# Two first-product blocks between the halves of G in the first batch, the gate's weights behind v, and a left-over pass whose strips hold column quarters

## The chip, the cores and the metric

The kernel runs on one core of one Trainium2 chip. The metric is the device time of one execution in microseconds. The core has a matrix engine (TensorE; PE for its matmuls and PEld for its weight loads in the profile), VectorE (DVE), ScalarE (ACT), GpSimd (POOL) and SyncE (SP), which issues nearly all of the transfers here.

## The reference

An attention with packed queries is followed by a mixture of experts with one expert per row.

```
p_packed = sm_attn(p, k, v)            # q, k, v: 8 batches x 8 heads x 576 x 64; p: 32 packed queries a head
x = sm_attn(q, p_packed, p_packed)     # each of the 576 rows attends to the 32 packed rows
x = x as 4608 rows x 512
e = argmax(x @ w_gate)                 # one of 8 experts a row
out[row] = gate_w[row] * sigmoid(x @ w_output_gate)[row, e] * (relu(x @ w1[e]) @ w2[e])
                                       # w1: 8 x 512 x 1024, w2: 8 x 1024 x 512
```

## The kernel before

Eight batches are worked through one after the other. For each of them `encode` computes the packed attention (scores `ps_s`, exponentials, their transposes `ps_a1T`, the product with v `ps_pp`), guesses one expert for the whole batch and loads its weights (`weights`); `route` computes the second attention up to its transposed weights, split into a high and a low part (`ah`, `al`), and the gate. `values_up` multiplies the packed values by the first weights of the guessed expert: G has two halves of 512 columns (`up(0)` and `up(1)`, 16 matmuls each), each lying in two PSUM banks (one for each group of heads), and `take_in` splits a bank into a high part on ScalarE (`Gh`, L76) and a low part on VectorE (`Gl`, L77). `ffn` then makes eight first-product blocks (`ps_h`, fc 0 to 7) of 128 rows of the hidden layer for each of two halves of the batch's rows. Blocks 0 to 3 read the first half of G, blocks 4 to 7 the second. Each is evicted as a rectified high part by ScalarE (L514) and a low part by VectorE (L517), and `product_out` multiplies by the second weights (`ps_o`, L556 and L571), which ScalarE and VectorE have split as well (L461, L463).

The order on every engine is written out by hand. `START` is a string of pieces done ahead of the first batch's `ffn`: `Y` and `y` step `encode`, `t` steps `route`, `W` steps `weights`, `G` steps `values_up`, digits are matmuls on zeros that keep TensorE busy, and `k`, `v`, `q` issue loads on SP's queue. `PLANS` has one string per batch; `8:WW` places two steps after the eighth step of that batch's `ffn`. In the first batch `values_up` gives way four times: after `up(0)`, after `up(1)`, and after either take-in. `START` has three of these steps (both products and the first take-in), and the plan's `1:G` does the second take-in behind block 0. PSUM has eight banks, four of which (tag "f") serve the warming matmuls, G of the first batch, the blocks `ps_h`, the outputs `ps_o` and the left-over pass. Before the second-layer weights are issued, GpSimd waits for the second chunk of the first ones (L172).

The loads are issued in the order of the string: k with the packed queries of the batch, then v, then q. Behind the second half of the first batch's k the gate's weights `wgo` (32 KB) are issued (L197, L198). They are first used in `encode(0)` at L274.

Rows whose expert is not the guessed one are left over. `first_leftover` treats one (row tile, quarter, expert) with 32 rows (`m` is 32) beside the last batch's `ffn`, at the letters `l` of the last plan; further ones go through a loop at the end, which runs no times with these inputs. With `m` = 32, `product` puts the 32-row partial products into four strips of 32 PSUM partitions, each strip with 512 columns and a fourth of the sum. The strips are added later, by the matrix `stack4`: for the hidden layer with eight products against it, which transpose at the same time (L687), and for the output with one more product (L697). Between the two stands the second layer's `product`. The row numbers (`ridi`) and scales (`vals`) are brought to 32 partitions by a product with `pick` (L643), and `scatter` writes 32 rows of 512 columns by an indirect transfer.

Of the kernel before, what the change touches and what calls it, by code (L numbers as in the profile page):

```python
# [19 lines left out]
P = 128  # L20
# [11 lines left out]
PLANS = ["1:G 4:WW 6:W 8:WW 9:tt 10:tWW 11:yy 12:Wyy 13:tt 14:ttty 15:ty 16:tyy 17:ty 19:yt 20:y 21:ryyr 22:yr 23:y "  # L32
# [9 lines left out]
def tile_packed_attn_then_moe(ctx, tc, qT, kT, v, pT, w_go, w1, w2, out):  # L42
# [131 lines left out]
    def fetch(x):  # L174

        queue = queues["kvq".index(x)]
        if not queue:
            return
        x, b, g = key = queue.pop(0)
        tag = "rq" if x == "q" else "raw"  # L180
        bufs = CFG[tag]
        if x == "v":
            t = sb.tile([P, T, NPAIR * D], F32, tag=tag, name="vt", bufs=bufs, **EVEN)
            if b == g == 0:
                after(nc.vector, t[0:1, 0, 0:1], loaded["k", 0, 0][0:1, 0, 0:1])
            nc.sync.dma_start(t, v[b, g])
        else:
            t = sb.tile([P, NPAIR, HS], F32, tag=tag, name=x, bufs=bufs, **EVEN)
            src = (kT if x == "k" else qT)[b, g]
            step = NPAIR // 2 if b == 0 else NPAIR  # L190
            for c in range(0, NPAIR, step):
                nc.sync.dma_start(t[:, c:c + step], src[:, c:c + step])
                if x == "k" and g == c == 0:
                    pt = sb.tile([P, NPAIR, NP], F32, tag="pt", name="pt", bufs=2)
                    nc.sync.dma_start(pt, pT[b])
                    loaded["p", b, g] = pt
        if key == ("k", 0, 1):  # L197
            nc.sync.dma_start(wgo, w_go)  # L198
        loaded[key] = t

# [268 lines left out]
    def values_up(b):  # L469

        w1s = W[b][0]
        ppT = packed[b]
        G[b] = []

        def up(n, tag):
            banks = [bank("ps_G", tag) for _ in range(NG)]
            by_head(banks, ppT, w1s[n * NPAIR:(n + 1) * NPAIR])
            return banks

        def take_in(banks):  # L480
# [6 lines left out]
        both = []  # L487
        for n in range(DF // BANK):
            both.append(up(n, "fa"[n] if b else "f"))
            if b == 0 or n:  # L490
                yield
        for banks in both:
            take_in(banks)
            yield

    def ffn(b):
        ah, al = A.pop(b)
# [83 lines left out]
    def leftover(nb=B, m=P):  # L581


        nq = P // m
        tags = dict(l_oh="raw", l_h="raw", l_some="row", l_a2="row", l_pp="row", l_o="ob", l_x="rq", l_hT="rq")

        def st(shape, nm, dt=F32, n=P):
            tag = tags.get(nm, nm)
# [44 lines left out]
        if m < P:  # L633
            here = st([Q], "l_q")
            nc.vector.tensor_reduce(here, oh.rearrange("p c q e -> p q c e"), axis=AX.XY, op=ALU.max)
            nc.vector.tensor_tensor(here, here, quarter[:, :, 0], ALU.mult)
            mine = st([1], "l_mine")
            nc.vector.tensor_reduce(mine, here, axis=AX.X, op=ALU.max)
            pick = st([m], "l_pick")
            nc.vector.tensor_scalar(pick, stack4, mine, None, ALU.mult)  # L640
            yield
            ps = bank("ps_lv", "f")[:m, :4]
            nc.tensor.matmul(ps, pick, vals, start=True, stop=True)  # L643
            vals = st([4], "l_valq", n=m)
            nc.vector.tensor_copy(vals, ps)
        ef = st([1], "l_ef", n=m)
        nc.vector.tensor_copy(ef, dec[:m, 0:1])
        nc.vector.tensor_tensor(ef, ef, vals[:, 0:1], ALU.not_equal)
        rid = st([1], "l_rid", n=m)
        nc.vector.scalar_tensor_tensor(rid, ef, no_row, vals[:, 2:3], op0=ALU.mult, op1=ALU.add)  # L650
        ridi = st([1], "l_ridi", I32, n=m)
        nc.vector.tensor_copy(ridi, rid)
        yield
        total = stack4 if m < P else ident
# [5 lines left out]
        for c in range(NPAIR):  # L660
            nc.scalar.copy(xT[:, c], pv[c])

        def product(ps, stat, wc):
# [10 lines left out]
        h = st([FC, P], "l_h")  # L674
        nf = BANK // P
        for n in range(DF // BANK):
            ps = bank("ps_lh", "f")
            yield from product(ps, xT, w1c[n * NG:(n + 1) * NG])
            nc.scalar.copy(h[:, n * nf:(n + 1) * nf], ps.rearrange("p (c n) -> p c n", n=P))
            yield  # L680
        hT = st([FC, m], "l_hT")
        for n in range(0, FC, BANK // m):
            fs = slice(n, min(FC, n + BANK // m))
            ps = bank("ps_lt", "f")
            pv = ps.rearrange("p (c n) -> p c n", n=m)[:, :fs.stop - fs.start]
            for c_ in range(fs.start, fs.stop):
                nc.tensor.matmul(pv[:, c_ - n], h[:, c_], total, start=True, stop=True)  # L687
            nc.scalar.activation(hT[:, fs], pv, AF.Relu)
        yield
        ps = bank("ps_lo", "f")  # L690
# [7 lines left out]
        ob = sb.tile([m, DM], F32, tag="ob", name="l_ob", bufs=CFG["ob"])  # L698
# [120 lines left out]
```

## Time and profile before

| | |
|---|---|
| median of 3 runs | 421.17 us (419.62 to 421.27) |
| profiled execution | 420.52 us |
| its span, first to last instruction | 418.8 us |
| mean granted TensorE clock | 0.993 of full speed |
| TensorE matmuls, busy | 404.1 us (96%) |
| VectorE, busy | 282.4 us (67%) |
| ScalarE, busy | 182.5 us (44%) |
| GpSimd, busy | 40.8 us (10%) |

The profiled execution is one of the kernel's executions, and its time is 1.7 us above its span. Sums over rows are made against 420.52. The times in all rows are microseconds from the start of the span.

### The profile page before, as it was taken

Reading aid. Unit: us, or ns where it says so; the run is one execution under the profiler, and the core shown is the slowest. Engines: PE = TensorE matmul, PEld = TensorE weight load, DVE = VectorE, ACT = ScalarE, POOL = GpSimd, SP = SyncE. Lnnn points to the kernel's source line nnn. Section 1 sums busy time; section 2 is a strip of 40 time slices with the busy share of each in tenths; the row PEclk is TensorE's granted clock in tenths of the full one; section 3 lists DMA queues with packets and bytes.
Section 4 is the critical chain, followed back from the end, with each engine's and each line's share of the span. In section 5 each row is a group of like instructions: output and inputs, shape, how many; then the busy total and the mean of one; then the engine's idle time right before and its main releaser. Section 6 shows DMA issues by size and latency. Waiting matters only on the chain.

```text
span 418.8 us, 9413 instructions
## 1 busy us (share of the span) xinstructions
PE 404.1 (96%) x3616; PEld 321.5 (77%) x3616; DVE 282.4 (67%) x810; ACT 182.5 (44%) x408; POOL 40.8 (10%) x36
## 2 busy tenths in 40 slices
PE   7979999899999999999999999999999999999994
PEld 4648877677868888788877888788977888798754
DVE  2659578585895776749774786749774786677610
ACT  2246425462467337342645337442645334533310
POOL 6000000260024200020002000020002000200010
PEclk9999999899999999999999999999999999999998
DMA  7999219920697079602992079602951077004801
GB/s 251 334 357 411 92 57 386 377 119 33 200 412 298 10 240 409 269 27 87 355 410 91 3 237 409 273 27 97 346 198 59 2 244 285 25 27 119 344 13 53
DMA packets 36686, 83.60 MB, mean 200 GB/s; under 512 B 3615, under 2 KB 16287, under 8 KB 36640
## 3 DMA queue, kind: packets, MB, share of 16 engines
q1 hardware_dynamic: 36608, 82.98, 54.2%
q8 instruction: 29, 0.48, 0.5%
q14 instruction: 17, 0.14, 0.1%
q0 software_dynamic: 32, 0.00, 0.0%
HBM read 67.76 MB, written 15.27 MB: 198 GB/s over the span
## 4 chain that ended last, share of the span: by engine, by line
PE 79%; DVE 1%; ACT 1%; issue 0%
PE ps_o L556 38%; PE ps_h L85 21%; PE ps_o L571 6%; PE ps_G L92 3%; PE ps_pp L92 2%; PE ps_s L92 2%; PE ps_s2T L92 2%; PE ps_a1T L240 1%; PE ps_lg L92 1%; ACT hT L514 1%; PE ps_lh L669 0%; PE ps_lo L669 0%; ACT a L231 0%; DVE Gl L77 0%; PE ps_lt L687 0%; PE ps_lg L85 0%
## 5 line engine op out<-in xcount | busy, mean ns | idle before, releaser
L556 PE MATMUL ps_o<-w2h,hT 128*128 128x512 f32 (+1 forms) x528 | 168.8, 391 | 0.1
L556 PEld LDWEIGHTS ps_o<-w2h,hT 128*128 128x128 f32 x528 | 98.2, 188 | 28.2 <-ACT Gh L76 5.0
L517 DVE SCALAR_TENSOR_TENSOR hT<-ps_h,hT 128x256 fp32r<-128x256 f32 x192 | 61.0, 352 | 65.4 <-ACT hT L514 65.0
L556 PE MATMUL ps_o<-w2l,hT 128*128 128x512 f32 (+1 forms) x264 | 101.4, 384 | 0.0
L85 PE MATMUL ps_h<-ah,Gh 128*128 128x256 f32 (+1 forms) x256 | 78.7, 308 | 1.2 <-DVE hT L517 0.7
L85 PE MATMUL ps_h<-al,Gh 128*128 128x256 f32 (+1 forms) x256 | 76.1, 297 | 0.0
L85 PE MATMUL ps_h<-ah,Gl 128*128 128x256 f32 (+1 forms) x256 | 76.0, 297 | 0.0
L514 ACT ACTIVATE hT<-ps_h 128x320 fp32r<-128x320 f32 (+1 forms) x128 | 51.4, 415 | 47.9 <-PE ps_h L85 47.2
L463 POOL TENSOR_TENSOR w2l<-wst,w2h 128x1024 fp32r<-128x1024 f32 x13 | 31.1, 2397 | 311.8 <-ACT w2h L461 281.7
L556 PEld LDWEIGHTS ps_o<-w2l,hT 128*128 128x128 f32 x264 | 49.7, 188 | 8.6
L85 PEld LDWEIGHTS ps_h<-ah,Gh 128*128 128x128 f32 x256 | 48.9, 191 | 6.2 <-DVE hT L517 1.8
L85 PEld LDWEIGHTS ps_h<-al,Gh 128*128 128x128 f32 x256 | 49.0, 191 | 0.2
L85 PEld LDWEIGHTS ps_h<-ah,Gl 128*128 128x128 f32 x256 | 49.0, 191 | 0.0
L538 ACT ACTIVATE ob<-ps_o,scm_all 128x512 f32<-128x512 f32 (+1 forms) x28 | 19.0, 680 | 37.2 <-PE ps_o L556 34.4
L461 ACT CAST w2h<-wst 128x1024 fp32r<-128x1024 f32 x32 | 33.4, 1069 | 3.2 <-PE ps_o L556 2.8
L463 DVE TENSOR_TENSOR w2l<-wst,w2h 128x1024 fp32r<-128x1024 f32 x19 | 23.2, 1220 | 6.3 <-ACT w2h L461 6.3
L77 DVE TENSOR_TENSOR Gl<-ps_G,Gh 128x512 fp32r<-128x512 f32 x32 | 20.1, 684 | 9.2 <-ACT Gh L76 9.1
L362 ACT CAST ah<-a2T 128x576 fp32r<-128x576 f32 (+1 forms) x18 | 11.2, 621 | 33.7 <-DVE a2T L356 33.7
L571 PE MATMUL ps_o<-w2h,hT 128*128 128x512 f32 x64 | 25.7, 401 | 0.1
L342 ACT ACTIVATE s<-s 128x576 f32<-128x576 f32 (+1 forms) x18 | 11.1, 629 | 29.9 <-DVE s L339 29.2
L571 PE MATMUL ps_o<-w2l,hT 128*64 128x512 f32 x64 | 23.9, 393 | 0.0
L231 ACT ACTIVATE a<-ps_s,nmx 128x288 f32<-128x288 f32 x32 | 15.8, 508 | 10.3 <-DVE nmx L226 9.5
(182 smaller groups left out, 446.0 us busy)
## 6 DMA issues: line engine op xcount, KB each, us to landing
w<-in_w_dram SPq DMA_DIRECT2D x36, 512.0 KB, 5.6
wst<-in_w_dram SPq DMA_DIRECT2D x36, 512.0 KB, 8.7
vt<-in_v_dram SPq DMA_DIRECT2D x16, 640.0 KB, 9.3
k<-in_kT_dram SPq DMA_DIRECT2D x14, 576.0 KB, 10.5
q<-in_qT_dram SPq DMA_DIRECT2D x14, 576.0 KB, 10.2
out_dram<-ob SPq DMA_DIRECT2D x31, 256.0 KB, 4.0
a_d<-a2T SPq DMA_DIRECT2D x16, 320.0 KB, 8.7
out_dram<-ob SPq DMA_DIRECT2D x10, 128.0 KB, 5.0
```

Of the source, the lines that this page charges most:

```text
L77: (lo_eng or nc.vector).tensor_tensor(lo, src, f(hi), ALU.subtract)
L85: res = nc.tensor.matmul(dst, a, m, start=j == 0, stop=j == len(seq) - 1)
L92: res = nc.tensor.matmul(dst, a, m, start=j == 0, stop=j == len(seqs[0]) - 1)
L231: nc.scalar.activation(a1[:, g, hf], s1[hf][g], AF.Exp, bias=nmx[g], scale=QK, accum_out=sm[:, g, hf:hf + 1])
L362: nc.scalar.copy(ah[:, g, ts], a2T[:, g, ts])
L461: nc.scalar.copy(hi, st)
L463: eng("w", b, j).tensor_tensor(lo, st, f(hi), ALU.subtract)
L514: nc.scalar.activation(hT[:, :n], ps, AF.Relu)
L517: nc.vector.scalar_tensor_tensor(hT[:, d0:d0 + s1 - s0], ps[:, s0:s1], 0.0, f(hT[:, s0:s1]), op0=ALU.max, op1=ALU.subtract)
L538: nc.scalar.activation(ob[:, cs], ps[:, cs], AF.Copy, scale=sc)
L556: nc.tensor.matmul(ps[:, cs], a, m[:, cs], start=fc == i == 0, stop=fc == FC - 1 and i == 2)
L571: nc.tensor.matmul(ps[:n], a, m, start=i == 0, stop=i == len(seq) - 1)
```

## The change

Three things are changed.

- In the first batch `values_up` now goes `up(0)`, take-in, `up(1)`, take-in, with a step after each. `START` has the first two, and the plan of the first batch has `2:GG` in place of `1:G`: the second product and its take-in stand behind blocks 0 and 1. The take-ins of this batch go by half banks: the first 256 columns of both banks, then the second 256. Other batches keep their order.
- The gate's weights are issued behind the second v load of the first batch instead of the second k load.
- In the left-over pass with 32 rows, `product` gives each strip of 32 partitions a quarter of the columns and the whole sum: four matmuls of 128 columns for each former one of 512. The hidden layer is rectified when it leaves PSUM, turned by two transposes of 128x128, and copied; the output needs no further product. `pick` now spreads row numbers and scales to all 128 partitions, each strip has its quarter's index added (`part`), and the scatter writes 128 pieces of 128 columns. The last step is one plan letter shorter.

```
-START = "kkvvqqkkYYYY1YY2YYY3YY4YYtYYWtttWYtttttttty6GGGvvqqkkvv"
+START = "kkvvqqkkYYYY1YY2YYY3YY4YYtYYWtttWYtttttttty6GGvvqqkkvv"
-PLANS = ["1:G 4:WW 6:W 8:WW 9:tt 10:tWW ...
+PLANS = ["2:GG 4:WW 6:W 8:WW 9:tt 10:tWW ...
...
-        if key == ("k", 0, 1):
+        if key == ("v", 0, 1):
             nc.sync.dma_start(wgo, w_go)
...
-        def take_in(banks):
+        def take_in(banks, parts=1):
+            new = []
             for ps in banks:
...
-                split(gh, gl, ps)
-                G[b].append((gh, gl))
+                new.append((gh, gl))
+            for x in range(parts):
+                cs = slice(x * BANK // parts, (x + 1) * BANK // parts)
+                for ps, (gh, gl) in zip(banks, new):
+                    split(gh[:, cs], gl[:, cs], ps[:, cs])
+            G[b].extend(new)
+        if b == 0:
+            for n in range(DF // BANK):
+                banks = up(n, "f")
+                yield
+                take_in(banks, 2)
+                yield
...
-            pick = st([m], "l_pick")
-            nc.vector.tensor_scalar(pick, stack4, mine, None, ALU.mult)
+            pick = st([Q, m], "l_pick")
+            nc.vector.tensor_scalar(pick, stack4.rearrange("p (o m) -> p o m", o=1).to_broadcast([P, Q, m]), mine, None,
+                                    ALU.mult)
+            nc.vector.tensor_tensor(here, iota[:, 0, 0:Q], quarter[:, :, 0], ALU.mult)
+            part = st([1], "l_part")
+            nc.vector.tensor_reduce(part, here, axis=AX.X, op=ALU.add)
...
+        if m < P:
+            nc.vector.scalar_tensor_tensor(rid, rid, float(Q), part, op0=ALU.mult, op1=ALU.add)
...
-                    nc.tensor.matmul(ps[i % nq * m:(i % nq + 1) * m], stat[:, i], wt[:, k], start=i < nq, stop=i >= n - nq)
+                    for q in range(Q) if wide else [0]:
+                        nc.tensor.matmul(ps[q * m:(q + 1) * m], stat[:, i], wt[:, k, q * P:(q + 1) * P] if wide else wt[:, k],
+                                         start=i == 0, stop=i == n - 1)
...
+            if wide:
+                yield from product(ps[:, :P], xT, w1c[n * NG:(n + 1) * NG])
+                nc.scalar.activation(h[:, n], ps[:, :P], AF.Relu)
...
+        if wide:
+            ps = bank("ps_lt", "f")[:, :FC * m]
+            for n in range(DF // BANK):
+                nc.tensor.transpose(ps[:, n * P:(n + 1) * P], h[:, n], ident)
+            nc.scalar.copy(hT.rearrange("p c n -> p (c n)"), ps)
...
-        if m < P:
-            parts = st([DM], "l_o")
-            nc.scalar.copy(parts, ps)
-            yield
-            ps = bank("ps_lo", "f")[:m]
-            nc.tensor.matmul(ps, total, parts, start=True, stop=True)
...
-        nc.gpsimd.indirect_dma_start(out=out[0:nb * S], out_offset=bass.IndirectOffsetOnAxis(ap=ridi, axis=0),
-                                     in_=ob, in_offset=None, bounds_check=nb * S - 1, oob_is_err=False)
+        n = ob.shape[1]
+        nc.gpsimd.indirect_dma_start(out=out[0:nb * S].rearrange("r (j n) -> (r j) n", n=n),
+                                     out_offset=bass.IndirectOffsetOnAxis(ap=ridi, axis=0),
+                                     in_=ob, in_offset=None, bounds_check=nb * S * DM // n - 1, oob_is_err=False)
```

## Rows read from the trace of the kernel before

**Rows 1.** The page: TensorE's busy time, and engines on the chain that ended last.

```profile
PE 404.1 (96%) x3616; PEld 321.5 (77%) x3616; DVE 282.4 (67%) x810; ACT 182.5 (44%) x408; POOL 40.8 (10%) x36
...
PE 79%; DVE 1%; ACT 1%; issue 0%
```

**Rows 2.** Timeline, TensorE, first batch: start, length, instruction, idle before and releaser.

```profile
21.89 1.06 PE L92 MATMUL ps_G<-w,ppT 64*32 64x512 f32 x8 [0.19 <-DMA w<-in_w_dram]
24.59 2.25 PE L92 MATMUL ps_G<-w,ppT 64*32 64x512 f32 x16 [1.64 <-DMA w<-in_w_dram]
...
28.68 0.39 PE L85 MATMUL ps_h<-ah,Gh 128*128 128x256 f32 x1 [0.22 <-DVE hT L517]
...
33.01 0.28 PE L85 MATMUL ps_h<-ah,Gl 128*128 128x256 f32 x1
33.41 0.50 PE L556 MATMUL ps_o<-w2h,hT 128*128 128x512 f32 x1
```

**Rows 3.** Timeline, TensorE's weight loads, the same stretch.

```profile
25.77 0.15 PEld L92 LDWEIGHTS ps_G<-w,ppT 64*32 64x32 f32 x8 [1.03 <-DMA w<-in_w_dram]
```

**Rows 4.** Timeline, ScalarE, first batch.

```profile
23.00 1.07 ACT L76 CAST Gh<-ps_G 128x512 fp32r<-128x512 f32 x2
27.79 0.38 ACT L514 ACTIVATE hT<-ps_h 128x256 fp32r<-128x256 f32 x1 [3.71 <-PE ps_h L85]
...
30.73 1.04 ACT L461 CAST w2h<-wst 128x1024 fp32r<-128x1024 f32 x1
...
41.22 0.51 ACT L231 ACTIVATE a<-ps_s,nmx 128x288 f32<-128x288 f32 x1
```

**Rows 5.** Timeline, VectorE, first batch.

```profile
14.51 0.19 DVE L274 TENSOR_TENSOR sums<-wgo,ps_cs 128x32 f32<-128x32 f32 x1 [0.54 <-PE ps_cs L268]
...
23.62 1.29 DVE L77 TENSOR_TENSOR Gl<-ps_G,Gh 128x512 fp32r<-128x512 f32 x2 [0.87 <-ACT Gh L76]
28.20 0.42 DVE L517 SCALAR_TENSOR_TENSOR hT<-ps_h,hT 128x256 fp32r<-128x256 f32 x1 [3.30 <-ACT hT L514]
...
31.80 1.22 DVE L463 TENSOR_TENSOR w2l<-wst,w2h 128x1024 fp32r<-128x1024 f32 x1 [0.51 <-ACT w2h L461]
32.94 1.41 DVE L517 SCALAR_TENSOR_TENSOR hT<-ps_h,hT 128x256 fp32r<-128x256 f32 x4
```

**Rows 6.** Chain of work that ended last, last batch: start, length, what.

```profile
388.74 0.99 PE ps_lh L669 x8
...
394.32 1.70 PE ps_lt L687 x16
...
404.98 0.98 PE ps_lo L697 x2
```

**Rows 7.** Timeline, GpSimd, first batch.

```profile
22.95 0.79 POOL L365 TENSOR_TENSOR al<-a2T,ah 128x288 fp32r<-128x288 f32 x1 [0.88 <-ACT ah L362]
```

**Rows 8.** Busy time of each engine from 34 to 45, TensorE's clock, transfers.

```profile
34.00:45.00 11.00, 11.00 (x54) 9.17 (x53) 10.66 (x26) 5.32 (x14) 0.00 (x0) 1.00 0.80 316
```

**Rows 9.** Timeline, TensorE, transposes and logits of the first batches.

```profile
41.73 1.03 PE L240 MATMUL ps_a1T<-ident,a 128*128 128x128 f32 x8
...
45.58 0.64 PE L92 MATMUL ps_lg<-a2T,pg 128*32 128x128 f32 x16
46.04 0.39 PE L85 MATMUL ps_lg<-a2T,pg 128*32 128x64 f32 x4
```

**Rows 10.** SP's queue: an issue in the timeline, and its wait, with total, times, longest.

```profile
10.76 0.33 SPq L192 DMA_DIRECT2D k<-in_kT_dram  x1
...
SPq L192 <- DMA vt<-in_v_dram: 1.8, 1, 1.8
```

**Rows 11.** Timeline, VectorE, start of the last batch's second half.

```profile
383.82 0.56 DVE L517 SCALAR_TENSOR_TENSOR hT<-ps_h,hT 128x256 fp32r<-128x256 f32 x2 [1.32 <-ACT hT L514]
```

**Rows 12.** The left-over product's weight loads: count, shortest, median and longest in ns.

```profile
L669 PEld LDWEIGHTS ps_lh<-w,l_x x16: 106/108/109, 388.7 to 390.8; 128*32 128x32 f32 x16
```

More of the change, by code (lines that the diff above doesn't have):

```diff
@@ L24 @@
                  "sub0.0.1", "al0.0.1"))
-START = "kkvvqqkkYYYY1YY2YYY3YY4YYtYYWtttWYtttttttty6GGGvvqqkkvv"
+START = "kkvvqqkkYYYY1YY2YYY3YY4YYtYYWtttWYtttttttty6GGvvqqkkvv"
 BESIDE = "8:ry 9:yrr 10:yrrrt 11:yr 12:wrr 13:wrqq 14:rkk 15:r "
 REST = "16:xr 17:x 18:r 19:xvv 20:x 22:x 24:x 25:xxw 26:ww 27:rw 28:r 30:r 31:rxg 32:xg 33:gw 34:ww"
-PLANS = ["1:G 4:WW 6:W 8:WW 9:tt 10:tWW 11:yy 12:Wyy 13:tt 14:ttty 15:ty 16:tyy 17:ty 19:yt 20:y 21:ryyr 22:yr 23:y "
+PLANS = ["2:GG 4:WW 6:W 8:WW 9:tt 10:tWW 11:yy 12:Wyy 13:tt 14:ttty 15:ty 16:tyy 17:ty 19:yt 20:y 21:ryyr 22:yr 23:y "
          "24:wt 25:wkkrr 26:tr 27:trr 28:drqq 29:r 30:t 31:g 32:gr 33:rg",
@@ L483, in take_in @@
                 gl = sb.tile([P, BANK], F32R, tag="Gl", name="Gl", bufs=4, **WIDE)
-                split(gh, gl, ps)
-                G[b].append((gh, gl))
[L487 to L490, printed above, removed]
+                new.append((gh, gl))
[7 more added lines that the diff above has]
+                banks = up(n, "f")
                 yield
-        for banks in both:
-            take_in(banks)
+                take_in(banks, 2)
+                yield
+        else:
+            both = [up(n, "fa"[n]) for n in range(DF // BANK)]
             yield
+            for banks in both:
+                take_in(banks)
+                yield
     def ffn(b):
@@ L581, in leftover @@
     def leftover(nb=B, m=P):
-        nq = P // m
-        tags = dict(l_oh="raw", l_h="raw", l_some="row", l_a2="row", l_pp="row", l_o="ob", l_x="rq", l_hT="rq")
+        tags = dict(l_oh="raw", l_h="raw", l_some="row", l_a2="row", l_pp="row", l_x="rq", l_hT="rq", l_pick="rq")
         def st(shape, nm, dt=F32, n=P):
@@ L661, in leftover @@
             nc.scalar.copy(xT[:, c], pv[c])
+        wide = m < P
         def product(ps, stat, wc):
@@ L673, in leftover @@
         yield
-        h = st([FC, P], "l_h")
         nf = BANK // P
+        h = st([FC // Q if wide else FC, P], "l_h")
         for n in range(DF // BANK):
             ps = bank("ps_lh", "f")
-            yield from product(ps, xT, w1c[n * NG:(n + 1) * NG])
-            nc.scalar.copy(h[:, n * nf:(n + 1) * nf], ps.rearrange("p (c n) -> p c n", n=P))
+            if wide:
+                yield from product(ps[:, :P], xT, w1c[n * NG:(n + 1) * NG])
+                nc.scalar.activation(h[:, n], ps[:, :P], AF.Relu)
+            else:
+                yield from product(ps, xT, w1c[n * NG:(n + 1) * NG])
+                nc.scalar.copy(h[:, n * nf:(n + 1) * nf], ps.rearrange("p (c n) -> p c n", n=P))
@@ L680, in leftover @@
             yield
         hT = st([FC, m], "l_hT")
[L682 to L688, printed above, removed]
+        if wide:
[3 more added lines that the diff above has]
+            nc.scalar.copy(hT.rearrange("p c n -> p (c n)"), ps)
+        else:
+            for n in range(0, FC, BANK // m):
+                fs = slice(n, min(FC, n + BANK // m))
+                ps = bank("ps_lt", "f")
+                pv = ps.rearrange("p (c n) -> p c n", n=m)[:, :fs.stop - fs.start]
+                for c_ in range(fs.start, fs.stop):
+                    nc.tensor.matmul(pv[:, c_ - n], h[:, c_], ident, start=True, stop=True)
+                nc.scalar.activation(hT[:, fs], pv, AF.Relu)
@@ L689, in leftover @@
         yield
-        ps = bank("ps_lo", "f")
+        ps = bank("ps_lo", "f")[:, :P if wide else DM]
         yield from product(ps, hT, w2c)
-        if m < P:
-            parts = st([DM], "l_o")
-            nc.scalar.copy(parts, ps)
-            yield
-            ps = bank("ps_lo", "f")[:m]
-            nc.tensor.matmul(ps, total, parts, start=True, stop=True)
-        ob = sb.tile([m, DM], F32, tag="ob", name="l_ob", bufs=CFG["ob"])
+        ob = sb.tile([P, P if wide else DM], F32, tag="ob", name="l_ob", bufs=CFG["ob"])
```

15 lines of the change are left out of this document (7 added, 8 removed).

## The prediction

> **What bounds the kernel now.** I read the page's engine table and chain first. TensorE is busy 404.1 of 418.8 us and holds 79% of the chain that ended last [rows 1]. So a change gains only what it takes off TensorE's own stream, in work or in idle time, and anything on the other engines counts only where TensorE waits for it. Two stretches are touched. In the first batch's start I read TensorE's timeline: two groups of first-weight products (`ps_G`, the two halves of G), then the eight first-product blocks of six matmuls, then the second product at 33.41 [rows 2]. TensorE idles 1.64 us ahead of the second half of G, for weights that are still in flight; the loads' timeline shows the other half of these weights arriving as late as 25.77 [rows 3]. ScalarE and VectorE have taken in the first half of G by 24.07 and 24.91 [rows 4, 5], so work is ready that the order in the code holds back. In the last batch I read the chain between 388 and 406: the left-over pass stands in it with every step, among them 16 small matmuls of 1.70 us and a pair of 0.98 us that do nothing but sum over four partial results [rows 6]. There every microsecond taken from TensorE should move the end.
>
> **The change, part 1: order in the first batch.** After it the first two blocks stand between the halves of G, and each half is taken in by half banks, both first halves ahead of both second halves. The first half of G ends on TensorE at 21.89 + 1.06 = 22.95 [rows 2]. ScalarE starts its take-in at 23.00 with two whole banks in 1.07 [rows 4]. A half bank has the form of the 128x256 eviction, 0.38 alone [rows 4], and by estimate 0.3 in a run (two whole banks overlap to 1.07). VectorE's half has about the length of its 128x256 step, 1.41 for four, so 0.35 each [rows 5]. First halves: ScalarE to 23.38 and 23.7, VectorE to about 23.8 and 24.2. The blocks also need the low part of the second group of activations from GpSimd, there at 22.95 + 0.79 = 23.74 [rows 7]. Block 0's first matmul can therefore start at 23.4, but its sixth needs the last low half, so it ends at about 24.4. One block is six matmuls at (33.01 - 28.68) / 35 = 0.124 [rows 2], 0.74, so block 1 ends at 25.1. The second half of G has its first weights from 24.59 and its last from 25.77 [rows 2, 3], so it runs 25.1 to 27.2 without the long wait. Block 2 follows at 27.2 where before it started at 28.68 [rows 2]: 1.45 us earlier.
>
> Next is the take-in of the second half, now four half-bank steps on either engine ahead of block 2's evictions in their queues: ScalarE 27.3 to 28.5, VectorE 27.7 to 29.15. Behind these wait block 2's and 3's evictions and the first weight cast. Blocks 2 and 3 end at 28.7, when the first halves are in (28.4); block 4 wants a PSUM bank. Before, block 2 waited until 28.68 for the eviction of block 0 (28.20 + 0.42 = 28.62) [rows 2, 5], so banks are handed on in the order in which they come free; by that order block 4 takes a bank of G's second half, free at 28.8, and the stall is 0.1. Blocks end at 31.8. The second product also needs the low part of the first second-layer weights. ScalarE's cast of them, before at 30.73 [rows 4], comes behind block 3's eviction, 29.1 to 30.15; VectorE's subtraction, before from 31.80 [rows 5], runs 30.2 to 31.4. The product can start at about 31.9 instead of 33.41: 1.5 earlier.
>
> Does it keep that? From 34 to 45 VectorE is busy 10.66 of 11 us [rows 8]. At three quarters of the second product TensorE turns the second batch's exponentials: the transposes start at 41.73 [rows 9], and the last exponential, which waits for maxima from VectorE, ends at 41.22 + 0.51 = 41.73 [rows 4]. So this stretch is already just in time, and it can come earlier only by what VectorE gains. VectorE does the evictions of blocks 0 and 1 in its old idle time of 3.30 ahead of 28.20 [rows 5] and pays about 0.2 for half banks; it comes out 1.3 to 1.4 earlier, TensorE 1.5, so a stall of 0.1 to 0.2 remains there. **I take 1.4 gained.** Bounds: at best the second half of G is tied to the weights alone (25.77 + 1.06 = 26.83, six blocks of 0.74 then give 31.3), 2.1 gained; at worst TensorE gets nothing and VectorE's extra steps, four of 0.35 against two in 1.29 for either half [rows 5], some 0.3, fall on its saturated stretch: 0.3 lost. I stay between them, nearer the better end, because each step of this chain has a row of its own.
>
> **Part 2: the gate's weights behind v.** One transfer of 32 KB is issued after the two v transfers instead of before. No engine waits for v's arrival in the rows, and the gate's weights are used only at 14.51, on VectorE [rows 5]. On SP's queue the two q transfers of either half and the second batch's k and packed queries now come behind it. A subtler cost: the second half of that k is issued at 10.76, when the wait for the first v transfer ended [rows 10]; it is the eighth transfer behind that one, so an issue seems to wait for the one eight before. With v one place earlier, the same issue would wait for the second v transfer, about 1.6 later. I cost it at nothing, since q and the first half of k are still in flight in front of it. If that cover is missing, second-batch scores come later, and up to 1.6 goes onto TensorE ahead of G. At the other end the first k loads could be freed of 32 KB: at most the issue time of one transfer, 0.4, is gained.
>
> **Part 3: the left-over pass.** The four partial sums no longer lie over the four strips of partitions; instead each strip gets a quarter of the columns and all of the sum.
> - The two final sum matmuls go: 0.98 [rows 6], and a ScalarE copy beside them.
> - The 16 summing matmuls of 1.70 [rows 6] become two 128x128 transposes. Eight of these took 1.03 [rows 9], so two cost 0.25 to 0.3: 1.4 gained.
> - The products: four steps (two of each layer) of 8 matmuls of 512 columns, 0.99 each [rows 6], become steps of 32 matmuls of 128 columns. The same form stands in the logits: 16 of them start at 45.58 and the next group at 46.04 [rows 9], 0.46 for 16, so 0.92 for 32. I take no change; bounds 0.3 gained and 0.4 lost over the four.
> - The row-number product has a 128-wide stationary: about 0.1 more, at a place where TensorE waits for an eviction anyway.
> - VectorE gets two small steps and a four times wider multiply ahead of block 0 of the last half, 0.5 by two steps of 0.19 like the small one at 14.51 [rows 5] and 0.1 for the width. There it stands idle 1.32 before 383.82 [rows 11], which covers them; uncovered they would cost their 0.5. One more step behind the row-number copy is another 0.19, between evictions.
> - The scatter has 128 rows of 512 B instead of 32 of 2 KB and is issued two plan steps earlier, some 5 us ahead of the last stores; nothing waits for it.
>
> Together 0.98 + 1.4 = **2.4 gained** (1.9 to 2.8). All around is TensorE's own chain, so it should reach the end.
>
> The Trainium skill speaks against this part. In "TensorE: Matmul & The Clock Gate", under Part 3, The mechanism, it says that a weight load overlaps running matmuls only where the row group differs; the four strips here share all 128 rows. It would make every added load a cost of its own. What that would give is the slower rival below; the logits' row speaks against it.
>
> **The sum.** 1.4 + 0 + 2.4 = 3.8 off the profiled execution's 420.52, of which 418.8 is the span: 416.7. The median of the three runs, 421.17, lies 0.65 above that execution, so I forecast 417.3.
>
> **The rivals.**
> 1. *Loads that are not hidden.* A 128x32 load takes 0.108 [rows 12]. If the 32 loads of a step ran alone, a step would take 32 x 0.108 + 0.92 = 4.4 instead of 1.0, four steps 13.5 more: with the other gains 421.2 + 9.7 = 430.9. It decides the sign once a load leaves over 0.03 uncovered (3.8 / 128). Against it: 16 loads alone would be 1.73, and the logits' 16 loads and matmuls took 0.46 together [rows 9]. A chance of 0.05.
> 2. *The first batch gives nothing back.* VectorE, saturated from 34 to 45 [rows 8], is the bound there, and the earlier start turns into a wait ahead of the transposes at 41.73, or the late k issue of part 2 eats it: only part 3 is left, 421.2 - 2.4 = 418.8, down to 420 if 1.4 is lost as well. For it: VectorE has hardly any idle time there. Against: the 3.30 ahead of it that the new order fills. Chance 0.18.
> 3. *Part 3 does not do what it says*: the summing work was hidden between other matmuls and its removal opens waits for evictions. Then only the 1.4 remain: 419.8. The chain shows it on the path with no gap on either side [rows 6], so 0.06.
>
> **How the numbers follow.** The forecast's own case (all three parts within their bounds) has 0.71, from 415.8 to 418.6. The range takes in rival 2's upper part: 415.6 to 419.4. Faster by over 0.5% (about what a measurement of this kernel can tell from no change) means below 419.06: the forecast and most of rival 2, 0.81. Within 0.5%: rival 3 and the rest of rival 2, 0.13. Slower: rival 1 and an unseen delay at the start, 0.06.
>
> **What would show it.** Right: no wait for weights ahead of the second half of G or one below 0.5; second product at 32 +- 0.4; the transposes of the second batch with a stall under 0.3; the left-over's product steps at 0.9 to 1.05 each, its transposes at 0.3 and no final sum. Wrong: a second product that starts after 33, weight loads of the quarter matmuls that stand in line, second-batch scores later than 17 to 19, or a new gap on TensorE behind the transposes.

## The result and the profile after

| | before | changed |
|---|---|---|
| median | 421.22 us | 416.08 us |
| lowest to highest | 419.49 to 422.29 | 415.37 to 418.92 |
| profiled execution, span | 420.52, 418.8 | 416.11, 414.3 |
| mean granted TensorE clock of that execution | 0.993 | 0.997 |

The ratio is 0.9896, with a 95% interval from 0.9873 to 0.9919: 1.04% faster. 417.3 had been forecast, from 415.6 to 419.4. The medians lie 5.14 apart, the means of the ten executions each (421.02 and 416.65) only 4.38.

To see where the 4.50 us of the two spans went I cut both executions at five instructions that both have: the starts of the first and the third batch's second scores (`ps_s2T`), of the first and the second batch's logits (`ps_lg`), and of the last eviction. The sums of the columns are the two spans.

| stretch | before | changed | difference |
|---|---|---|---|
| start to the first batch's second scores (`ps_s2T`, 15.37 and 15.97) | 15.37 | 15.97 | +0.60 |
| to the first batch's logits (`ps_lg`, 45.58 and 44.68): part 1 lies here | 30.21 | 28.71 | -1.50 |
| to the second batch's logits at 78.81 and 78.02 | 33.23 | 33.34 | +0.11 |
| to the third batch's second scores at 99.72 and 97.45 | 20.91 | 19.43 | -1.48 |
| to the last eviction (413.32 and 408.15): part 3 lies here | 313.60 | 310.70 | -2.90 |
| to the end | 5.48 | 6.15 | +0.67 |

So the stretches of parts 1 and 3 gained about what was forecast, and 1.48 came from a place that the change does not touch.

The changed kernel's page has these engine totals (compare [rows 1]):

```profile
PE 399.4 (96%) x3696; PEld 321.1 (78%) x3696; DVE 282.4 (68%) x817; ACT 181.7 (44%) x411; POOL 41.1 (10%) x36
```

TensorE runs 80 instructions more and is busy 4.7 us less. Next its timeline in the first batch (columns as in [rows 2]):

```profile
15.97 1.20 PE L92 MATMUL ps_s2T<-q,ppT 64*32 64x288 f32 x32
...
19.23 1.16 PE L92 MATMUL ps_s<-k,pt 64*32 64x288 f32 x19 [1.34 <-issue]
...
21.63 1.70 PE L92 MATMUL ps_G<-w,ppT 64*32 64x512 f32 x16
23.80 0.39 PE L85 MATMUL ps_h<-ah,Gh 128*128 128x256 f32 x1 [0.47 <-ACT Gh L76]
...
25.65 2.12 PE L92 MATMUL ps_G<-w,ppT 64*32 64x512 f32 x16
29.58 0.39 PE L85 MATMUL ps_h<-ah,Gh 128*128 128x256 f32 x1 [0.18 <-DVE Gl L77]
...
32.55 0.48 PE L565 MATMUL ps_o<-w2h,hT 128*128 128x512 f32 x1
```

The wait of 1.64 ahead of the second half of G [rows 2] is gone: it starts without one at 25.65, behind the two blocks. But a wait for weights is left inside it, and makes it 2.12 long. The timeline of the weight loads (compare [rows 3]) shows the second eight of them 0.91 late:

```profile
26.71 0.15 PEld L92 LDWEIGHTS ps_G<-w,ppT 64*32 64x32 f32 x8 [0.91 <-DMA w<-in_w_dram]
```

Besides it, 0.47 and 0.18 are left for the take-ins. ScalarE and VectorE (compare [rows 4, 5]) show the take-ins by half banks, four steps of VectorE in 1.62:

```profile
23.38 0.65 ACT L76 CAST Gh<-ps_G 128x256 fp32r<-128x256 f32 x2
24.24 0.70 ACT L76 CAST Gh<-ps_G 128x256 fp32r<-128x256 f32 x2 [0.22 <-DVE Gl L77]
```

```profile
23.78 1.62 DVE L77 TENSOR_TENSOR Gl<-ps_G,Gh 128x256 fp32r<-128x256 f32 x4 [0.43 <-ACT Gh L76]
25.46 0.42 DVE L526 SCALAR_TENSOR_TENSOR hT<-ps_h,hT 128x256 fp32r<-128x256 f32 x1
...
28.23 1.62 DVE L77 TENSOR_TENSOR Gl<-ps_G,Gh 128x256 fp32r<-128x256 f32 x4 [1.63 <-ACT Gh L76]
```

The 0.22 between ScalarE's pairs is one that was not in the forecast: the profile names VectorE's steps on the same banks (L77) as what the second halves wait for. In the chain of the last batch (compare [rows 6]) the left-over pass now reads:

```profile
386.35 1.01 PE ps_lh L685 x32
387.36 1.07 PE ps_h L85 x6
388.43 1.01 PE ps_lh L685 x32
...
391.90 0.22 PE ps_lt L706 x2
392.12 2.29 PE ps_o L580 x10
394.42 1.01 PE ps_lo L685 x32
395.43 1.60 PE ps_o L565 x6
397.03 1.01 PE ps_lo L685 x32
398.04 10.09 PE ps_o L565 x66
...
408.15 0.47 ACT ob L547
```

The last eviction of the kernel before stands at 413.32:

```profile
413.32 0.47 ACT ob L538
```

Each product step of 32 small matmuls takes 1.01, against 0.99 to 1.06 for 8 large ones. The transposes take 0.22 for 1.70, and the last output product runs through without a break.

The remaining 1.48 goes with TensorE's clock. Before the change TensorE waits in the third batch's scores for 1.66 us, and then the granted clock stands at 0.50, the lower of its two levels (1.2 of 2.4 GHz); in the changed kernel's execution the same wait is 1.19 and the clock stays at 1.00. First the waits and the ends of the stretch, in TensorE's timelines, of the kernel before and of the changed one; the same 16 matmuls of the logits take 1.08 and 0.64:

```profile
77.57 1.31 PE L92 MATMUL ps_s<-k,pt 64*32 64x288 f32 x16 [1.66 <-DVE Gl L77]
78.81 1.08 PE L92 MATMUL ps_lg<-a2T,pg 128*32 128x128 f32 x16
...
99.72 1.20 PE L92 MATMUL ps_s2T<-q,ppT 64*32 64x288 f32 x32
```

```profile
76.77 1.31 PE L92 MATMUL ps_s<-k,pt 64*32 64x288 f32 x16 [1.19 <-DVE Gl L77]
78.02 0.64 PE L92 MATMUL ps_lg<-a2T,pg 128*32 128x128 f32 x16
...
97.45 1.20 PE L92 MATMUL ps_s2T<-q,ppT 64*32 64x288 f32 x32
```

Then the busy times of the two microseconds behind them, before and after; the clock is the third figure from the right:

```profile
79.00:81.00 2.00, 2.00 (x23) 1.75 (x18) 0.00 (x0) 0.24 (x1) 1.69 (x1) 0.50 1.03 416
```

```profile
79.00:81.00 2.00, 2.00 (x18) 2.00 (x18) 0.49 (x2) 1.11 (x5) 1.84 (x1) 1.00 1.05 392
```

Neither clock belongs to its kernel for good. The mean clock of single executions ranges from 0.988 to 1.000 in the changed kernel and from 0.984 to 1.000 in the one before. So the experiments below are compared twice: by the ratio of their times, and at equal clock. For the latter the 205 executions of all kernels whose clock is on record were fitted by one time for each kernel plus a common slope on the mean granted clock; one execution of the whole-bank kernel, 420.79, is left out as slow. The slope is 0.30 us for each 0.001 of clock, and single executions scatter around the fit by 0.73.

The comparison at equal clock has two limits. The mean clock also counts the tail: in all 14 profiles the clock falls to 0.50 some 2 to 5 us behind TensorE's last matmul, where TensorE has no work left. That lowers the mean by 0.001 to 0.005, on average by 0.0022 in the four profiles without part 3 and by 0.0035 in the ten with it; so at equal clock the kernels with part 3 may look some 0.4 better than they are. And a gain that comes through the clock itself cannot show at equal clock.

| kernel | ratio to before (95% interval) | at equal clock, us (standard error) |
|---|---|---|
| changed, both measurements together | 0.9896 (0.9873 to 0.9919) and 0.9868 (0.9829 to 0.9907) | -4.46 (0.20) |
| part 1 alone | 0.9951 (0.9928 to 0.9974) | -1.47 (0.23) |
| part 2 alone | 0.9996 (0.9972 to 1.0019) | +0.07 (0.23) |
| part 3 alone | 0.9949 (0.9929 to 0.9970) | -2.59 (0.23) |
| parts 1 and 3 | 0.9886 (0.9858 to 0.9913) | -4.73 (0.31) |
| changed, whole-bank take-ins, both together | 0.9900 (0.9862 to 0.9937) and 0.9912 (0.9879 to 0.9946) | -4.36 (0.20) |
| changed, old order, half banks kept | 0.9939 (0.9909 to 0.9969) | -2.63 (0.24) |
| changed, wait in the third batch filled | 0.9897 (0.9867 to 0.9927) | -4.31 (0.23) |
| before, the same wait filled | 1.0009 (0.9985 to 1.0034) | +0.30 (0.23) |
| changed, waits of the start filled | 0.9886 (0.9847 to 0.9925) | -4.47 (0.31) |
| changed, strips one after the other | 1.0063 (1.0031 to 1.0094) | +1.56 (0.27) |

### The profile page after: what moved, and what is told of

It is laid out like the page before. It is cut to its first block, busy times and chain, and to the rows that moved or that the text cites. A ratio compares the mean times of both kernels' runs of the same rounds, so it can differ in the third digit from the quotient of the medians.

```text
span 414.3 us, 9584 instructions
## 1 busy us (share of the span) xinstructions
PE 399.4 (96%) x3696; PEld 321.1 (78%) x3696; DVE 282.4 (68%) x817; ACT 181.7 (44%) x411; POOL 41.1 (10%) x36
## 4 chain that ended last, share of the span: by engine, by line
PE 78%; DVE 1%; ACT 1%; issue 0%
PE ps_o L565 38%; PE ps_h L85 21%; PE ps_o L580 6%; PE ps_G L92 3%; PE ps_pp L92 2%; PE ps_s L92 2%; PE ps_s2T L92 2%; PE ps_a1T L240 1%; PE ps_lg L92 1%; ACT hT L523 1%; PE ps_lh L685 0%; PE ps_lo L685 0%; ACT a L231 0%; DVE Gl L77 0%; PE ps_lg L85 0%; DVE al L365 0%
## 5 line engine op out<-in xcount | busy, mean ns | idle before, releaser
L77 DVE TENSOR_TENSOR Gl<-ps_G,Gh 128x512 fp32r<-128x512 f32 (+1 forms) x36 | 20.5, 624 | 10.5 <-ACT Gh L76 10.3
L76 ACT CAST Gh<-ps_G 128x512 fp32r<-128x512 f32 (+1 forms) x36 | 17.1, 548 | 9.4 <-PE ps_G L92 8.9
```

Of the source, the lines that this page charges most:

```text
L76: (hi_eng or nc.scalar.copy)(hi, src)
L77: (lo_eng or nc.vector).tensor_tensor(lo, src, f(hi), ALU.subtract)
```

## The experiments

**The parts, one by one.** Theory: part 1 is worth 1.4 to 1.5, part 3 2.4 to 2.8, and part 2 delays the start, since the changed kernel's first scores ended 0.6 later. Rival: part 2 is nothing, and the late start belonged to that execution.

*Part 1 alone*, on the kernel before:

```
-START = "...tttttttty6GGGvvqqkkvv"
+START = "...tttttttty6GGvvqqkkvv"
-PLANS = ["1:G 4:WW ...
+PLANS = ["2:GG 4:WW ...
+                take_in(banks, 2)
```

> Part 1 alone on the kernel before (order in the first batch with half banks; the gate's weights stay behind k, the left-over pass stays). Theory: the new order is worth 1.4 to 1.5 on its own, and the changed kernel showed only 0.86 at the second product because the gate's weights behind v delayed its first scores: second product at 31.9 to 32.0, 0.3% to 0.4% below the kernel before, or up to 0.8% where the half clock at 78 goes away as it did in the changed kernel. Rival: the order alone is worth only the 0.86 seen there: second product at 32.5, 0.2% below.

*Part 3 alone*: the functions `leftover` and `scatter` of the changed kernel in the kernel before.

> Part 3 alone on the kernel before (left-over pass). Theory: the 2.8 us between the blocks of the last batch and its last output come from here, so 0.65% below the kernel before, with the half clock at 78 to 82 unchanged. Rival: part of it is given back in the tail, where the changed kernel took 5.7 from the last eviction to the end instead of 5.0: then 0.5% below.

*Part 2 alone*:

```
-        if key == ("k", 0, 1):
+        if key == ("v", 0, 1):
             nc.sync.dma_start(wgo, w_go)
```

> Part 2 alone on the kernel before (gate's weights behind v). Theory: it lets v's transfers run into those of the first k, whose last piece lands at 8.2 instead of 7.6: everything on TensorE from the first maxima on is 0.6 to 1.0 later, 0.15% to 0.25% above the kernel before. Rival: the later landing belonged to that one execution; the last k lands at 7.6 and the time is within 0.1%.

*Parts 1 and 3 without part 2*:

```
-        if key == ("v", 0, 1):
+        if key == ("k", 0, 1):
             nc.sync.dma_start(wgo, w_go)
```

> Parts 1 and 3 without part 2: the changed kernel with the gate's weights back behind k. Theory (part 2 costs 0.6 to 1.0): 0.2% below the changed kernel, 1.25% below the kernel before, last piece of the first k at 7.6. Rival (part 2 costs nothing): the same 1.04% as the changed kernel.

Parts 1 and 3 came out at -1.47 and -2.59 at equal clock; their sum, 4.06, and part 2's +0.07 lie within the errors of the whole, -4.46. Part 3 can be read in the traces without the clock: from the first product step of the left-over pass to the last eviction it is 24.52 to 24.58 in the four profiles without part 3 and 21.80 to 21.82 in the nine with it (the strips one after the other left aside), so 2.7 to 2.8. Nothing of it is given back behind: from the last eviction to the end it is 5.5 to 6.3 without and 5.6 to 6.4 with part 3. The ratio alone, 0.5%, would not have told the theory's 0.65% from its rival's 0.5%.

The second product in the execution of part 1 alone started at 33.16, later than either side had said, but the first half of G had ended at 23.38 + 1.06 = 24.44 there, because everything ahead of it came later (the half clock at the start, below). What tells the orders apart is the distance from that end. Taken off it are the wait ahead of the second half of G and that half's own length, which holds the waits inside it; the last column is the rest:

| kernel | end of the first half of G | second product | distance | second half: wait, length | rest |
|---|---|---|---|---|---|
| before | 22.95 | 33.41 | 10.46 | 1.64, 2.25 | 6.57 |
| part 2 alone (old order) | 24.05 | 33.99 | 9.94 | 0.44, 2.93 | 6.57 |
| part 3 alone (old order) | 25.90 | 34.99 | 9.09 | 0.29, 2.23 | 6.57 |
| before, later wait filled (below) | 23.44 | 34.47 | 11.03 | 2.23, 2.23 | 6.57 |
| old order, half banks (below) | 26.78 | 36.45 | 9.67 | 0.34, 2.25 | 7.08 |
| part 1 alone | 24.44 | 33.16 | 8.72 | 0, 1.63 | 7.09 |
| parts 1 and 3 | 23.02 | 31.75 | 8.73 | 0, 1.64 | 7.09 |
| changed | 23.33 | 32.55 | 9.22 | 0, 2.12 | 7.10 |
| changed, waits of the start filled (below) | 23.63 | 31.97 | 8.34 | 0, 1.24 | 7.10 |
| new order, whole banks, first and second time (below) | 23.00, 25.47 | 32.36, 34.22 | 9.36, 8.75 | 0, 1.69 and 0, 1.09 | 7.67, 7.66 |

With the old order the distance hangs on how late the second half of the weights is, which differs from one execution to the next. With the new order the wait ahead of the product is gone, and what is left inside it is between nothing (a length of 1.24) and 0.9 (a length of 2.12). The waits of the second half of G show it, in TensorE's timelines of part 3 alone (weights late already for the first half, which waits 1.46), of the kernel before with its later wait filled, and of the changed kernel with the start filled:

```profile
23.57 1.06 PE L92 MATMUL ps_G<-w,ppT 64*32 64x512 f32 x8 [1.46 <-DMA w<-in_w_dram]
24.84 1.06 PE L92 MATMUL ps_G<-w,ppT 64*32 64x512 f32 x8 [0.20 <-DMA w<-in_w_dram]
26.19 2.23 PE L92 MATMUL ps_G<-w,ppT 64*32 64x512 f32 x16 [0.29 <-DMA w<-in_w_dram]
```

```profile
25.67 2.23 PE L92 MATMUL ps_G<-w,ppT 64*32 64x512 f32 x16 [2.23 <-DMA w<-in_w_dram]
```

```profile
25.96 1.24 PE L92 MATMUL ps_G<-w,ppT 64*32 64x512 f32 x16
```

So the distance is 9.09 to 11.03 in the four profiles of the old order with whole banks, 10.13 in the mean, and 8.34 to 9.22 in the seven of the new order with half banks, 8.74 in the mean: 1.4 gained. The second half with its wait is 1.9 shorter in the mean, and the rest is 0.5 longer. So by this sum (an estimate, no run shows it) the old order would be the shorter one if the weights were in ahead of time.

Part 2 does nothing that can be measured, and the theory of a delay falls. The issue of the second batch's k does come later, as the prediction reckoned: SP's queue issues its packed queries at 10.29 and its second half at 11.93 instead of 10.76 [rows 10]:

```profile
4.71 0.80 SPq L198 DMA_DIRECT2D wgo<-in_w_go_dram  x1
...
10.29 0.33 SPq L195 DMA_DIRECT2D pt<-in_pT_dram  x1
11.93 0.33 SPq L192 DMA_DIRECT2D k<-in_kT_dram  x1
```

But the scores that need it start 19.23 - 15.97 = 3.26 behind the second scores with part 2, and in the kernel with parts 1 and 3 alone, where nothing of this is moved, 18.92 - 15.66 = 3.26 as well. In the other profiles it is 2.3 to 3.7 without part 2 and 2.4 to 3.3 with it. The cover held.

**Which half of part 1 gains.** Theory: the order gains by covering the wait for the weights, and the half banks hide the split. Rivals: the half banks do not matter; or they alone do it.

*Whole-bank take-ins in the new order*:

```
-                take_in(banks, 2)
+                take_in(banks)
```

> The changed kernel with whole-bank take-ins in the first batch (the new order stays). Theory (the half banks hide the split behind the blocks): block 0 waits for both whole banks, about 0.6 later, and block 4 waits again behind the second half of G; second product 0.6 to 1.0 later than in the changed kernel, 0.15% to 0.25% above it. Rival (the second product is set by its first weights and evictions, so the split does not matter): the same time as the changed kernel, 1.04% below the kernel before.

*Old place of the second half, half banks kept*:

```
-START = "...tttttttty6GGvv...     PLANS = ["2:GG 4:WW
+START = "...tttttttty6GGGvv...    PLANS = ["1:G 4:WW
```

> The changed kernel with the old place of the second half of G (directly behind the first half, its take-in behind block 0), half-bank take-ins kept. Theory (the order is what gains, by covering the wait for the weights): the wait of 0.5 to 1.6 ahead of the second half of G is back, and 1.2 to 1.6 of the gain is lost: 0.65% below the kernel before. Rival (the half banks alone start the blocks early): 0.9% to 1.0% below.

*Whole-bank take-ins once more, and the changed kernel beside them*:

> Whole-bank take-ins again, since six executions left open whether half banks matter. Theory (by the trace its logits of the second batch came 0.3 to 0.8 later behind the first batch's second scores than with half banks): 0.1% to 0.15% above the changed kernel of this call. Rival: no difference.

> The changed kernel once more, beside the others on one chip. Theory (all parts add up, about 4.2 at equal clocks): 0.99 to 0.9915 of the kernel before. Rival (its first measurement had luck with the clock): 0.992 or more.

Without the order, half banks are worth nothing: -2.63, which is part 3's -2.59; in the table above they even make the rest 0.5 longer (7.08 for 6.57). With the order they are worth 0.57 at the second product: the rest is 7.66 and 7.67 with whole banks and 7.09 to 7.13 in all seven profiles with half banks. The trace of the first kernel with whole banks shows where, with two waits at block 0, 0.69 and 0.22, where the changed kernel had 0.47:

```profile
23.69 0.38 PE L85 MATMUL ps_h<-ah,Gh 128*128 128x256 f32 x1 [0.69 <-ACT Gh L76]
...
24.42 0.38 PE L85 MATMUL ps_h<-ah,Gl 128*128 128x256 f32 x1 [0.22 <-DVE Gl L77]
...
32.36 0.50 PE L565 MATMUL ps_o<-w2h,hT 128*128 128x512 f32 x1
```

From the second scores to the next logits (the first batch's own, though the expectation above calls them the second's) the two whole-bank executions take 29.01 and 28.82 (15.50 to 44.51 and 17.55 to 46.37), the seven with half banks 28.17 to 28.71. The 0.57 reaches the logits, and 0.11 of it is given back in the next stretch (33.34 for 33.23). So the order is the larger part of part 1's gain, and the half banks are some 0.5 of it in the traces. The times do not resolve 0.5: -4.36 against -4.46, each to 0.20, and beside each other 0.9912 against 0.9868 with intervals that overlap. The changed kernel itself came out at 0.9868 there, so its first measurement was no stroke of luck.

**The clock.** Theory: the half clock behind the wait in the third batch costs the kernel before more often than the changed one, and filling the wait with matmuls on zeros saves it. The matmuls write columns of a PSUM bank that nothing else uses.

```
...
+            if b == 2 and hf == 0:
+                for _ in range(4):
+                    nc.tensor.matmul(s1[0][0][:, BANK - P:], blank, blank, start=True, stop=True)
...
```

> The changed kernel with four matmuls on zeros (some 0.9 us) in the wait between the two halves of the third batch's scores at 75.6 to 76.8; they write unused columns of a bank. Theory (in about half of the executions TensorE's granted clock falls to half for some 4 us behind this wait, and the changed kernel met that less often than the kernel before): the mean clock is 0.997 or more in nearly all executions, the slow ones near 418 are gone, 0.2% below the changed kernel, 1.25% below the kernel before. Rival (the clock falls elsewhere, or for another reason): clocks from 0.988 to 1.0 as before and no gain.

> The kernel before with the same four matmuls in the same wait (1.66 us there at 76 to 77.6). Theory (half clock behind this wait costs the kernel before about 1.1 us on average): clocks of 0.997 or more, 0.25% to 0.3% below the kernel before. Rival (the clock falls elsewhere, or what is left of the wait, 0.7, is enough): no gain, clocks as before.

The theory falls as to the gain. The wait is filled and the clock stands at 1.00 behind it in both profiles, but the kernels do not get faster. A gain through the clock has to be read from the ratios: 0.9897 beside the changed kernel's 0.9896, and 1.0009 for the kernel before. The 0.25% to 0.3% expected there lie outside its interval; the 0.2% expected of the changed kernel lie inside and are not ruled out. The mean clocks scatter from 0.987 to 0.999 as before, and their averages, 0.9941 and 0.9938, are no higher than without the filling, 0.9949 and 0.9944. The changed kernel with the filling, timeline of TensorE and busy times:

```profile
76.34 1.16 PE L224 MATMUL ps_s<-blank 128*128 128x128 f32 x8
77.43 0.71 PE L92 MATMUL ps_s<-k,pt 64*32 64x288 f32 x16
```

```profile
10.00:12.00 2.00, 2.00 (x12) 2.00 (x11) 0.40 (x1) 0.88 (x4) 0.00 (x0) 0.50 1.01 386
76.00:78.00 2.00, 2.00 (x40) 1.15 (x24) 1.12 (x2) 0.26 (x1) 0.00 (x0) 1.00 1.12 398
```

The half clock is at 10 to 12 in this execution. In the 14 profiles of this study it stands there, between 8 and 16, in seven (five of the first eleven, not four as the expectation below has it), and behind the third batch's wait in four, in two of them at both places. Ahead of the early place TensorE waits 1.5 for the first exponentials, and up to 1.5 for k. So I filled those waits too, with a new theory:

```
...
+            if b == 0:
+                for _ in range((3, 5)[hf]):
+                    nc.tensor.matmul(fill[:, :P], blank, blank, start=True, stop=True)
```

> The changed kernel with matmuls on zeros in two waits of the first batch's start: three behind the first half of the first scores and five behind the second (8.9 to 10.4, while the first maxima and exponentials are made). Theory (the half clock seen between 8 and 15 in four of the eleven profiles comes from these waits, and it is the larger part of what scatters the time): clocks of 0.997 or more in nearly all executions, none above 417, 0.2% to 0.25% below the changed kernel. Rival (TensorE's clock in this stretch does not set the time, since VectorE, ScalarE and loads do): clocks higher, time the same. Other rival: clocks scatter as before.

```profile
8.72 1.38 PE L224 MATMUL warm<-blank 128*128 128x128 f32 x10
10.29 0.71 PE L114 MATMUL warm<-blank 128*128 128x128 f32 x4 [0.19 <-ACT a L237]
```

```profile
10.00:12.00 2.00, 1.66 (x12) 1.31 (x12) 0.68 (x2) 1.69 (x8) 0.00 (x0) 1.00 1.02 387
78.00:80.00 2.00, 2.00 (x24) 1.76 (x17) 0.00 (x0) 0.00 (x0) 1.60 (x1) 0.50 1.05 392
```

In this execution the start keeps its clock, and the half clock shows at the other place. The ratio, 0.9886 beside 0.9868 for the changed kernel, shows no gain, and six executions with clocks from 0.991 to 0.999 don't show whether they became higher. Both fillings in one kernel were not tried, so whether the scatter can be removed stays open. What the half clock costs where it happens can be read. From the second batch's logits at 78 to the next second scores the ten executions without it took 19.40 to 19.46, and the four with it 20.64 to 20.93 (before, part 1, changed again, start filled), 1.2 to 1.5 more.

At the start it costs as much, which speaks against the rival that the clock does not set the time there. From the first matmul behind the wait for the exponentials to the first batch's second scores it is 5.56 or 5.57 in the seven profiles at full clock and 6.76 to 7.14 in the seven with half clock, 1.2 to 1.6 more. The changed kernel begins this stretch at 10.40 and has its second scores at 15.97; the second whole-bank execution begins it at 10.41, with the same wait ahead, and has them at 17.55:

```profile
10.40 0.71 PE L114 MATMUL warm<-blank 128*128 128x128 f32 x4 [1.50 <-ACT a L231]
```

```profile
10.41 0.71 PE L114 MATMUL warm<-blank 128*128 128x128 f32 x4 [1.50 <-ACT a L231]
...
17.55 1.20 PE L92 MATMUL ps_s2T<-q,ppT 64*32 64x288 f32 x32
```

What decides whether the clock falls stays open: all profiles but the filled one wait 1.50 there, and six of these 13 keep the clock.

**The order of the strips.** The forecast's slower rival was that weight loads for the four strips are not hidden. To see what hides them, the matmuls of a step were put in another order, all eight of a strip before the next strip:

```
-                    for q in range(Q) if wide else [0]:
-                        nc.tensor.matmul(ps[q * m:(q + 1) * m], stat[:, i], ...
+                for q in range(Q) if wide else [0]:
+                    for i in range(2 * j, 2 * j + 4):
+                        nc.tensor.matmul(ps[q * m:(q + 1) * m], stat[:, i], ...
```

> The changed kernel with the quarter-column products of the left-over pass in another order: all eight matmuls of a step and strip one after the other, then the next strip; same work, same loads. Theory (the strips run beside each other only where neighbours in the stream lie in different strips; the loads are hidden there): a step takes 32 x 0.107 = 3.4 instead of 1.0, four steps 9.7 more, 2.3% slower than the changed kernel. Rival (the order inside a step is free): 1.0 a step, no change. By the first rival of the prediction (each load a cost of its own in any order) the changed kernel's own steps would have been 4.4, and this one no slower than it.

The chain of this kernel:

```profile
386.63 2.39 PE ps_lh L685 x32
...
390.10 2.39 PE ps_lh L685 x32
...
397.48 2.39 PE ps_lo L685 x32
...
401.47 2.39 PE ps_lo L685 x32
```

A step takes 2.39, against 1.01 with neighbours in different strips; four of them make 5.5 more, and the time at equal clock is 6.0 above the changed kernel (+1.56 against -4.46). The theory has the right direction and too high a price: 0.075 for a load and a matmul in one strip instead of 0.107. Whether the loads or the matmuls stand in line within a strip, this run does not separate. The first rival of the prediction is refuted by the changed kernel's own 1.01. The Trainium skill ("TensorE: Matmul & The Clock Gate", Part 3, The mechanism) lets weight loads overlap running matmuls only across row groups. All strips here use all 128 rows, and the loads are hidden all the same (32 loads and 32 matmuls in 1.01, 0.032 for a pair), so the measurement decides against that sentence for column strips.

## Why the prediction held, step by step

- **Part 1, 1.4.** Measured alone 1.47 (0.23). Its steps, counted from the end of the first half of G: block 0 was forecast 0.45 behind it and came 0.47 behind it; the second half of G 2.15 and came 2.32, where a weight load of block 0 waits 0.16 for VectorE, whose half-bank step took 0.41 and not 0.35; block 4's stall 0.1, measured 0.18; the second product 8.95, measured 9.22 in the changed kernel and 8.34 to 9.22 over the profiles, as the last weights were in time or not. The stall of 0.1 to 0.2 that I put ahead of the second batch's transposes did not come: they start 8.28 behind the product (40.83), before 8.32. The term was right in the mean for a reason that I had only half: I took one execution's wait of 1.64 for the wait, and it is a draw between 0.3 and 2.2; and the wait inside the product, which I counted as over, was still 0.91.
- **Part 2, nothing.** Measured +0.07 (0.23). The issue that I expected about 1.6 later came 1.2 later, and what stood in front of it covered it.
- **Part 3, 2.4.** Measured alone 2.59 (0.23), and 2.7 to 2.8 in the traces from the first product step to the last eviction. Mis-sized were two terms. The transposes took 0.22, a saving of 1.48 instead of 1.4. The final sum took 0.98 itself, but from the first output product to the last eviction the chain is 1.18 shorter (13.71 against 14.89, from 394.42 and 398.41), so a broken stream had cost about 0.2 more than the piece in it. The product steps came out at 1.01, as the logits' row had said within a tenth.
- **The sum.** 3.8 forecast, 4.38 measured between the means, 4.46 (0.20) at equal clock, 5.1 between the medians. Part 3's 0.3 to 0.4 above its forecast make up half of the 0.6; the rest lies within the errors. That the median fell 1.2 below the forecast is for the larger part luck: the medians of the ten executions lie 0.8 further apart than their means. The clock was missing from the working: I never asked what the profiled execution's half clock at 79 to 82 was worth, nor whether it belongs to the kernel. It made 1.48 of the 4.50 between the two profiles. That it favoured the changed kernel in the times is not shown: mean clocks were 0.9944 before and 0.9949 in the changed kernel over 82 and 16 executions, which is 0.15 by the slope.
- **The signs.** The second product at 32 +- 0.4 was missed with 32.55, and the changed kernel again had it at 33.71, past the 33 named as a sign of being wrong. Of the 0.65 by which 32.55 misses 31.9, 0.38 is a late start (the first half of G ended at 23.33 and not at 22.95) and 0.27 the wait inside the second half. The 33.71 is a late start alone: the first half ended at 24.90, and the distance, 8.81, is below the forecast's 8.95. A time from the start of the span was the wrong yardstick. No wait was left ahead of the second half of G, as forecast; the one inside it was not looked for.
- **The rivals.** Unhidden loads: no (1.01 a step). VectorE as the bound in the first batch: no, the next logits came 1.5 earlier with everything else. Part 3 hidden: no. The start came 0.60 later and the tail took 0.67 more in the profiled execution. Both are scatter: the first batch's second scores start between 15.37 and 15.97 in the seven profiles that keep the clock there and between 16.28 and 17.98 in the seven that don't, and the start of the last eviction lies 5.5 to 6.4 ahead of the end.

No version beat the changed kernel clearly. Leaving part 2 out (-4.73 against -4.46, errors 0.31 and 0.20) is not resolved.

## What to carry to other kernels

Where a product waits for its second load, put work between that needs only the first; but size the gain over several executions, since a wait for a load is a draw and the new order's worth is that it matters less. Look for what is left of it in the timeline of the weight loads too: a product that starts without a wait can hold one. A sum over strips of partial results can be spared by giving each strip its own columns and the whole sum: with four times the matmuls a step took 1.01 for 0.99 here as long as neighbours in the stream lay in different strips, and 2.39 with neighbours in the same one. And compare the granted clock of two profiles stretch by stretch before putting a difference down to the change.

## What was not expected of the hardware

- TensorE's clock fell to its lower level behind waits of 1.49 to 1.66 us inside an otherwise busy stream in four executions, at 1.2 to 1.5 us each, and at the start in seven of 14, at 1.2 to 1.6. Part 3 alone and the old order with half banks waited 1.64 at the first of these places and kept their clock there.
- A pair of weight load and matmul with 128 columns on a 128x32 strip took 0.032 us with neighbours in other strips and 0.075 with neighbours in the same one.
- The weights' second half kept the old order waiting between 0.3 and 2.2 us ahead of its product in different executions of the same stretch of code.
